# First five units of an attention and expert kernel: a new order of the work, other numbers of warming products, and the gate's tables on GpSimd

## The chip, the cores and the metric

The kernel runs on one core of one Trainium2 chip. A core has a matrix engine (TensorE, PE in the profile; the loading of its weights is a row of its own, PEld), a vector engine (VectorE, DVE), an engine for activations (ScalarE, ACT), a general engine (GpSimd, POOL) and one that mostly issues transfers (SyncE, SP). The metric is the device time of one execution in microseconds, as a median over runs.

## The reference

Eight batches of twelve heads of attention over 448 positions with 64 dimensions, in float32, then a layer of experts with one expert for each token. Cut to what matters:

```python
q_n, k_n = rmsnorm(q, g_q), rmsnorm(k, g_k)          # x / sqrt(mean(x*x) + 1e-6) * g
scores = (q_n @ k_n.T) / sqrt(64)                    # for each batch and head
attn = softmax(scores)
x = (attn @ v) laid out as 3584 tokens x 768
logits = x @ w_gate + modality_bias[modality_id]     # 8 experts
e = argmax(logits); gate_w = softmax(logits)[e]
out = gate_w * (relu(x @ w1[e]) @ w2[e])             # w1[e]: 768 x 1024, w2[e]: 1024 x 768
```

## The kernel before, in words

**Units.** The attention is cut into 48 units, each two heads of one batch. For a unit: its q and k are loaded (`load`); ScalarE squares them and VectorE sums the squares (`sq`, function `sumsq`); ScalarE, with GpSimd, makes the reciprocal roots (`rs`, function `rstd`, for several units at a time); the norms scale q and k (`norm`, one operation each); TensorE transposes them (`tr`, L750), and ScalarE and VectorE write the transposed q and k apart into a high and a low part, some of which SP moves to other partitions with transfers of 112 KB (L763). Then TensorE makes approximate products for the maxima (`sa`, seven of them, one for each of 128 rows; L822, L827), VectorE takes the row maxima, TensorE transposes these (`mt`, L838), and a transfer puts them beside the low part of q. The score products proper (`st`, L855, seven with two or four instructions each) subtract the maximum at once, ScalarE takes the exponential, GpSimd and VectorE sum parts of it (`csum`), and TensorE multiplies with the values (`av`, L894, four columns of a unit, two in one step and two singly). Later follow the row sums by TensorE (`sums`, L909), the gate's logits (`gates`, L916), their transposes (`recips`, L928) and the output's transposes (`xt`, L951).

**Steps.** The order of the work is written out. A step n counts seven to a unit: at step n = 7u + j TensorE makes `st` number j of unit u. The loop starts at step -22, and until step 0 there is no `st`, only preparation. Everything else has a step of its own: a default distance from the unit's first step (`PLAN['sa']` 14 steps ahead, for example), or a step in `PLAN['first']`, which holds exceptions, most of them for the units at the start. `when` (L1141) looks them up. In a step the loop (from L1171) issues, in this order: the warming products, `st`, `sa`, and (before step 0) two more warming calls, `av`, `sums`, `gates`, `tr`, `mt`; then the evacuations of what was made in earlier steps; squares, roots, sums, norms, loads. An engine takes its own instructions in the order in which they were issued, and each transfer stands in the queue of the engine that issues it, most of them in SP's.

**Warming.** `warm(n)` (L1093) makes n products of a constant 128 by 128 matrix with another, both float32, into a bank that nothing reads. How many calls it makes ahead of a step is in `PLAN['warm']`; `PLAN['warmn']` adds two after the `sa` of every step before step 0.

**The gate's tables.** `gate_consts` (L148) makes eleven small tables from the loaded modality numbers, the bias and four index patterns: 112 by 256 elements in the three large ones. They are first used in `route`, for the first batch, long after the start. In the kernel before, its operations are deferred: they go into a list (`slow`) after step 6, from which `pump` lets one or two be issued at certain points of a step.

**Transfers of the start.** At step -4 the loop issues the values of units 0 and 1 (`load_v`), the gate's weights, modality numbers and bias (`load_gate`), and a fill of the list of tokens in memory (`l_d`, 224 KB of zeros). From step 6 the values of unit i + 2 are loaded at the end of unit i.

**Norms.** A norm runs on GpSimd unless `PLAN['nv']` names it; it names the q norm of unit 0 and the k norm of unit 2, which run on VectorE.

After the attention follows the layer of experts in slots of 256 tokens, from about 600 us on. The change does not touch it.

Of the kernel before, what the change touches and what calls it, by code (L numbers as in the profile page):

```python
# [13 lines left out]
ALU = mybir.AluOpType  # L14
# [5 lines left out]
NT, DM, DFF, NE = 3584, 768, 1024, 8  # L20
# [46 lines left out]
def kernel(  # L67
# [69 lines left out]
    def load_gate():  # L137
        with nc.allow_non_contiguous_dma(reason="small gate tables"):
            for half in range(2):
                SY.dma_start(wg[64 * half : 64 * half + 64, :, 8 * half : 8 * half + 8],  # L140
                             w_gate.rearrange("(j h p) e -> h p j e", h=2, p=64)[half])
            SY.dma_start(modr, mod_id.bitcast(I32).rearrange("(b p w) -> p b w", b=B, p=CP))
        SY.dma_start(
            bia.rearrange("p m e -> p (m e)"),
            mod_bias.rearrange("m e -> (m e)").unsqueeze(0).to_broadcast([CP, 2 * NE]),
        )

    def gate_consts():  # L148
# [497 lines left out]
    if True:  # L646
# [406 lines left out]
        P = PLAN  # L1053
# [117 lines left out]
        for n in range(P["start"], NJ * NU):  # L1171
# [71 lines left out]
            if done and len(routed) < B - 1 and done[-1] >= (NP * len(routed) + 5) // 4:  # L1243
# [6 lines left out]
                    slow.append(("exp", lambda b=b: put_all(b)))  # L1250
                if b == NB1 - 1:
                    slow.append(("exp", tables1))
            if n == -4:
                load_v(0)
                load_v(1)
                load_gate()
                SY.dma_start(l_d.rearrange("(p r) w -> p (r w)", p=128), zt)
# [191 lines left out]
```

## Time and profile before

| | |
|---|---|
| median of three runs | 1127.89 us (1124.01 to 1129.05) |
| profiled execution | 1126.66 us |
| its span in the profile | 1124.8 us |
| first product of any kind | 1.50 us |
| first transpose (unit 0) | 9.88 us |
| step 0, first `st` of unit 0 | 42.16 us |
| first `st` of unit 1, 2, 3 | 50.47, 66.78, 77.48 us |
| last `st` instruction | 576.2 us |
| PE busy | 1074.1 us (95%) |
| VectorE, ScalarE, GpSimd busy | 863.4, 821.5, 659.5 us |

The span runs from the first to the last instruction. A busy TensorE is one with an instruction in it; at half clock the same work is busy twice as long, so the granted clock has to be read beside it. "Idle before" is time in which the engine had nothing in it, with what ended it behind the arrow. A float32 product leaves two records; a score product in the engine's reduced format leaves one.

### The profile page before, as it was taken

The page shows a single profiled execution, that of the slowest core. Times are in us where ns is not written, and L with a number is a line of the kernel's source. Part 1 is how long each engine was busy: PE and PEld are TensorE (multiplying, and loading weights), DVE is VectorE, ACT ScalarE, POOL GpSimd, SP SyncE. Part 2 cuts the span into 40 slices and gives each one's busy share as a digit, 9 for nine tenths or more (in the row PEclk, how much of TensorE's full clock was granted, in tenths as well). Part 3 has the DMA queues.
Part 4 walks back from the last instruction along what each step waited for, and adds up shares of the span by engine and source line. Part 5 has one row for each costly group of instructions (what it writes and reads, how often), then busy time and mean ns, then how long its engine had stood idle before and what let it go on. Part 6 is the DMA issues. An engine that isn't in the chain of part 4 may idle for free.

```text
span 1124.8 us, 19920 instructions
## 1 busy us (share of the span) xinstructions
PE 1074.1 (95%) x6678; PEld 837.5 (74%) x6678; DVE 863.4 (77%) x1604; ACT 821.5 (73%) x1545; POOL 659.5 (59%) x658
## 2 busy tenths in 40 slices
PE   7899999999999999998999999999999999999993
PEld 6655555555555555554569989999999999999991
DVE  4677788888889877899699977667777677776770
ACT  5678888878778787876677577667876678766870
POOL 4477677778777688787865474354234432445440
PEclk7999999999999999999999999999999999999997
DMA  6656676677666777665833202111170111111360
GB/s 169 150 137 163 147 180 167 158 172 172 154 169 147 172 161 182 146 145 111 239 124 92 48 29 66 29 58 57 43 267 29 57 58 43 33 40 57 100 207 8
DMA packets 127969, 131.79 MB, mean 117 GB/s; under 512 B 68891, under 2 KB 122607, under 8 KB 126320
## 3 DMA queue, kind: packets, MB, share of 16 engines
q1 hardware_dynamic: 110212, 88.58, 33.5%
q0 software_dynamic: 17616, 41.80, 11.8%
q8 instruction: 57, 0.93, 0.4%
q14 instruction: 56, 0.46, 0.1%
q10 hardware_dynamic: 28, 0.01, 0.0%
HBM read 148.74 MB, written 22.38 MB: 152 GB/s over the span
## 4 chain that ended last, share of the span: by engine, by line
PE 75%; DVE 11%; DMA 7%; ACT 2%; issue 2%; POOL 1%; SPq 1%; ACTq 0%; DVEq 0%; POOLq 0%
PE ph L485 18%; PE py L515 16%; PE av L894 12%; PE st L855 12%; PE sa L827 5%; DMA lt<-l_d,tb_li 4%; PE tr L750 3%; DVE w1w L52 2%; DVE at_hlw L52 2%; PE xt L951 2%; PE sm L909 2%; PE px L468 2%; DMA w1w<-xw 1%; DVE xw L52 1%; DVE w2lw L52 1%
## 5 line engine op out<-in xcount | busy, mean ns | idle before, releaser
L485 PE MATMUL ph<-xw,w1w 128*128 128x256 f32 x2016 | 247.6, 285 | 3.0 <-DVE hlw L52 2.3
L485 PEld LDWEIGHTS ph<-xw,w1w 128*128 128x128 f32 x2016 | 245.3, 193 | 5.0 <-DVE hlw L52 2.5
L52 DVE TENSOR_REDUCE at_hlw<-sa 128x1 f32<-128x448 f32 x336 | 206.6, 617 | 44.4 <-PE sa L827 25.5
L52 DVE TENSOR_TENSOR w1w<-r,w1w 128x256 fp32r<-128x256 f32 x360 | 221.4, 672 | 13.3 <-ACT w1w L52 13.3
L52 ACT CAST w1w<-r 128x256 fp32r<-128x256 f32 x360 | 225.3, 732 | 0.5 <-DVE tb_t L53 0.4
L855 PE MATMUL st<-w1w 128*128 128x448 f32 (+1 forms) x480 | 175.5, 415 | 1.6 <-ACT r2w L52 1.6
L52 ACT ACTIVATE r2w<-st 128x448 f32<-128x448 f32 x168 | 90.9, 543 | 49.7 <-PE st L855 42.0
L52 ACT ACTIVATE hhw<-ph 128x512 fp32r<-128x512 f32 x56 | 33.5, 598 | 124.5 <-PE ph L485 124.5
L827 PE MATMUL sa<-w1w 128*128 128x448 f32 (+1 forms) x288 | 110.9, 386 | 14.1 <-DVE at_hlw L52 7.1
L855 PEld LDWEIGHTS st<-w1w 128*128 128x128 f32 (+1 forms) x480 | 84.8, 190 | 44.2 <-ACT r2w L52 21.8
L52 POOL TENSOR_TENSOR r2w<-r2w 128x448 f32<-128x448 f32 (+1 forms) x72 | 82.9, 1151 | 57.6 <-DVE r2w L52 18.5
L515 PE MATMUL py<-w2lw,hhw 128*128 128x384 f32 x448 | 114.0, 335 | 0.0
L52 ACT ACTIVATE at_w2lw<-st 128x448 f32<-128x448 f32 x168 | 90.9, 543 | 23.3 <-PE st L855 17.3
L52 ACT CAST w1w<-xw 64x448 fp32r<-64x448 f32 x188 | 105.3, 561 | 2.0
L855 PE MATMUL st<-w1w,w2ha 65*128 65x448 f32 x288 | 100.7, 370 | 1.8 <-DMA w1w<-xw 1.7
L52 POOL TENSOR_TENSOR xrw<-r,at_hlw 112x512 f32<-112x512 f32 x94 | 96.9, 1050 | 1.0 <-PE tr L750 0.7
L52 POOL DMA_INDIRECT out_dram<-yw,lb_oi x22 | 25.3, 1152 | 122.2 <-ACT yw L52 112.3
L515 PEld LDWEIGHTS py<-w2lw,hhw 128*128 128x128 f32 x448 | 80.9, 188 | 0.0
L52 DVE SCALAR_TENSOR_TENSOR hlw<-ph,hhw 128x512 fp32r<-128x512 f32 x56 | 38.7, 690 | 53.4 <-ACT hhw L52 53.4
L827 PEld LDWEIGHTS sa<-w1w 128*128 128x128 f32 (+1 forms) x288 | 55.3, 192 | 27.4 <-DVE at_hlw L52 13.0
L52 POOL TENSOR_TENSOR r2w<-r2w,at_w2lw 64x448 f32<-64x448 f32 (+1 forms) x48 | 55.3, 1152 | 30.3 <-DVE r2w L52 11.3
L52 POOL DMA_INDIRECT xrw<-x_d,lb_x2i x24 | 30.3, 1261 | 67.0 <-DMA xrw<-x_d,lt 63.4
(296 smaller groups left out, 2284.9 us busy)
## 6 DMA issues: line engine op xcount, KB each, us to landing
w1w<-xw SPq DMA_DIRECT2D x312, 112.0 KB
r<-in_q_dram SPq DMA_DIRECT2D x48, 224.0 KB
r<-in_k_dram SPq DMA_DIRECT2D x48, 224.0 KB
w2ha<-xw SPq DMA_DIRECT2D x72, 112.0 KB
x_d<-at_w2hb SPq DMA_DIRECT2D x8, 672.0 KB
x_d<-yw SPq DMA_DIRECT2D x8, 672.0 KB
r2w<-in_v_dram SPq DMA_DIRECT2D x48, 96.0 KB
at_w2lw<-in_v_dram SPq DMA_DIRECT2D x48, 96.0 KB
```

The costliest lines, as they stand in the source:

```text
L52: return fn(*a, **kw)
L468: PE.transpose(ps[:, i, 128 * t : 128 * t + 128], xr[t][:, 2 * g + i], idn)
L485: PE.matmul(ps[:, i], lhsT=lt_, rhs=rt_[:, c], start=n == 0, stop=n == 17)
L515: PE.matmul(ps[n][:, :384], lhsT=lt_[:, j, 128 * t : 128 * t + 128], rhs=rt_[:, 384 * n : 384 * n + 384], start=j == 0 and m == 0, stop=j ...
L750: PE.transpose(sp[:, c], src[:, c], idn[:CP, :CP])
L827: PE.matmul(ps[:, :S], lhsT=t["qq"][r, h, a : a + 128], rhs=t["kk"][h][r], start=True, stop=True)
L855: PE.matmul(ps[:, :S], lhsT=l, rhs=t["qq"][:, h] if first else t["ql"][:, h], start=first and (j != 3 or h == 0), stop=not first and (j != ...
L894: PE.matmul(t["av"][64 * h : 64 * h + 64, :S], lhsT=vv[r, u % 3, j], rhs=t["p"][r, j], start=c == 0, stop=c == 3)
L909: PE.matmul(R[g][32 * i : 32 * i + 32, :S], lhsT=sel[:, m], rhs=T[u + i // 2]["cs"][:, i % 2], start=m == 0, stop=False, tile_position=(0, ...
L951: PE.transpose(ps[:CP, 128 * c : 128 * c + 128], T[u]["xt"][:, c * CP : (c + 1) * CP], idn)
```

## The change

It replaces two lines of the plan and edits two functions:

- The steps of `PLAN['first']` for units 0 to 5 are laid out anew. Squares, roots and norms of units 0 to 2 shift by up to five steps; their transposes by at most one; `sa` of units 0 and 1 comes one step earlier; for units 2 to 5 `sa`, `tr` and `mt` get explicit steps, of which both transposes of unit 3 (step 7 instead of 0 and 4) and `sa` of unit 3 (step 10 instead of 7) move most.
- `PLAN['warm']` has 168 calls instead of 32, 163 of them before step 0, and 55 + 22 + 7 + 3 + 1 in steps -22 to -18.
- `PLAN['nv']` is empty: all norms run on GpSimd.
- The loads of the start have steps of their own: the values of unit 0 at step -9, of unit 1 at step 1, the gate's loads at -7, the fill of `l_d` at 4.
- `gate_consts` runs on GpSimd, issued as a whole at step 3.

```diff
-PLAN = {... 'first': {('sq', 0): -22, ('sk', 0): -22, ('nk', 0): -21, ('nq', 0): -20, ('sq', 1): -20, ('sk', 1): -20, ('sq', 2): -19, ('sk', 2): -19, ('nk', 1): -18, ('nq', 1): -18, ('tk', 0): -18, ('tq', 0): -18, ('sa', 0): -14, ('tk', 1): -13, ('tq', 1): -11, ('sa', 1): -7, ('mt', 0): -6, ('tk', 2): -8, ('tq', 2): -8, ('nq', 2): -14, ('nk', 2): -14, ('nq', 3): -2, ('nk', 3): -1, ('sq', 3): -8, ('sk', 3): -8, ('sq', 4): -9, ('sk', 4): -9, ... ('tq', 3): 4, ('mt', 1): 0, ('nq', 5): 10, ... ('rs', 0): -21, ('rs', 2): -18, ... ('rs', 5): -7, ('mt', 2): 8, ... ('sa', 5): 22, ('rs', 7): 0, ('rs', 8): 6, ('mt', 4): 22, ('nk', 4): 4, ('ld', 9): 6, ('tk', 5): 15}, ... 'warm': {5: 2, -6: 16, -12: 4, -7: 2, -9: 4, -21: 4}, 'warmn': 2, ... 'nv': [(2, 1), (0, 0)], ...}
+PLAN = {... 'first': {('sq', 0): -22, ('sk', 0): -21, ('nk', 0): -19, ('nq', 0): -18, ('sq', 1): -20, ('sk', 1): -19, ('sq', 2): -19, ('sk', 2): -18, ('nk', 1): -16, ('nq', 1): -13, ('tk', 0): -18, ('tq', 0): -17, ('sa', 0): -15, ('tk', 1): -13, ('tq', 1): -11, ('sa', 1): -8, ('mt', 0): -6, ('tk', 2): -9, ('tq', 2): -9, ('nq', 2): -13, ('nk', 2): -10, ('nq', 3): -2, ('nk', 3): -3, ('sq', 3): -13, ('sk', 3): -11, ('sq', 4): -10, ('sk', 4): -9, ... ('tq', 3): 7, ('mt', 1): 2, ('nq', 5): 13, ... ('rs', 0): -20, ('rs', 2): -16, ... ('rs', 5): -5, ('mt', 2): 9, ... ('sa', 5): 23, ('rs', 7): 8, ('rs', 8): 16, ('mt', 4): 24, ('nk', 4): -1, ('ld', 9): 6, ('tk', 5): 14, ('sk', 5): -14, ('tk', 3): 7, ('tk', 4): 9, ('nk', 5): 7, ('sq', 5): -14, ('mt', 3): 17, ('nq', 4): 1, ('sa', 4): 17, ('tq', 4): 12, ('sa', 3): 10, ('sa', 2): 1, ('tq', 5): 18}, ... 'warm': {-22: 55, -21: 22, -20: 7, -19: 3, -18: 1, -16: 8, -15: 3, -13: 14, -10: 9, -9: 1, -8: 6, -6: 19, -4: 8, -3: 6, -2: 1, 5: 3, 7: 2}, 'warmn': 2, ... 'nv': [], ... 'lv': (-9, 1), 'lg': -7, 'lz': 4, 'gc': 3}
...
     def gate_consts():
-        V.tensor_copy(out=m1, in_=modr.rearrange("p b (c w) -> p (b c) w", w=2)[:, :, 0])
-        V.tensor_scalar(out=m0, in0=m1, scalar1=-1.0, scalar2=1.0, op0=ALU.mult, op1=ALU.add)
+        GP.tensor_copy(out=m1, in_=modr.rearrange("p b (c w) -> p (b c) w", w=2)[:, :, 0])
+        GP.tensor_scalar(out=m0, in0=m1, scalar1=-1.0, scalar2=1.0, op0=ALU.mult, op1=ALU.add)
...
-            if n == -4:
-                load_v(0)
-                load_v(1)
+            for u in range(2):
+                if n == P["lv"][u]:
+                    load_v(u)
+            if n == P["lg"]:
                 load_gate()
+            if n == P["lz"]:
                 SY.dma_start(l_d.rearrange("(p r) w -> p (r w)", p=128), zt)
+            if n == P["gc"]:
+                gate_consts()
...
-            if i == 0:
-                slow += deferred(gate_consts)
```

The other nine operations of `gate_consts` change their engine in the same way.

More of the change, by code (lines that the diff above doesn't have):

```diff
@@ L33 @@
 ET = mybir.EngineType
-PLAN = {'rtj': 6, 'rushat': 36, 'av': (1, 1, 4, 6), 'xt': 4, 'xte': (2, 5), 'sm': 2, 'la': 6, 'rc': 9, 'csv': (1,), 'csj': (3, 6), 'csd': (1, 1), 'cse': (2, 1), 'sa': 14, 'mt': 6, 'tk': 21, 'tq': 18, 'nq': 26, 'nk': 26, 'sk': 49, 'sq': 50, 'rs': 48, 'ld': 58, 'first': {('sq', 0): -22, ('sk', 0): -22, ('nk', 0): -21, ('nq', 0): -20, ('sq', 1): -20, ('sk', 1): -20, ('sq', 2): -19, ('sk', 2): -19, ('nk', 1): -18, ('nq', 1): -18, ('tk', 0): -18, ('tq', 0): -18, ('sa', 0): -14, ('tk', 1): -13, ('tq', 1): -11, ('sa', 1): -7, ('mt', 0): -6, ('tk', 2): -8, ('tq', 2): -8, ('nq', 2): -14, ('nk', 2): -14, ('nq', 3): -2, ('nk', 3): -1, ('sq', 3): -8, ('sk', 3): -8, ('sq', 4): -9, ('sk', 4): -9, ('sq', 6): -6, ('sk', 6): -4, ('sk', 7): -7, ('sq', 8): 5, ('sk', 8): 5, ('nk', 7): 15, ('nq', 9): 31, ('tq', 3): 4, ('mt', 1): 0, ('nq', 5): 10, ('mt', 8): 50, ('rs', 0): -21, ('rs', 2): -18, ('nq', 8): 35, ('rs', 5): -7, ('mt', 2): 8, ('nq', 7): 18, ('mt', 5): 30, ('sk', 9): 15, ('tk', 9): 43, ('mt', 6): 36, ('nq', 6): 13, ('sa', 5): 22, ('rs', 7): 0, ('rs', 8): 6, ('mt', 4): 22, ('nk', 4): 4, ('ld', 9): 6, ('tk', 5): 15}, 'rs0': {0: 0, 2: 1, 5: 0, 7: 0, 8: 2}, 'sastep': 1, 'start': -22, 'warm': {5: 2, -6: 16, -12: 4, -7: 2, -9: 4, -21: 4}, 'warmn': 2, 'early': 1, 'late0': 1, 'pmp0': 2, 'ramp': 10, 'pmp': (0, 0, 1, 1, 1, 0, 1), 'nv': [(2, 1), (0, 0)], 'pmpa': (1, 0, 1, 0, 1, 1, 1), 'rush': (1, 1, 1), 'ps': [], 'pa': [], 'rtr': 6, 'sml': 4}
@@ new lines @@
+PLAN = {'rtj': 6, 'rushat': 36, 'av': (1, 1, 4, 6), 'xt': 4, 'xte': (2, 5), 'sm': 2, 'la': 6, 'rc': 9, 'csv': (1,), 'csj': (3, 6), 'csd': (1, 1), 'cse': (2, 1), 'sa': 14, 'mt': 6, 'tk': 21, 'tq': 18, 'nq': 26, 'nk': 26, 'sk': 49, 'sq': 50, 'rs': 48, 'ld': 58, 'first': {('sq', 0): -22, ('sk', 0): -21, ('nk', 0): -19, ('nq', 0): -18, ('sq', 1): -20, ('sk', 1): -19, ('sq', 2): -19, ('sk', 2): -18, ('nk', 1): -16, ('nq', 1): -13, ('tk', 0): -18, ('tq', 0): -17, ('sa', 0): -15, ('tk', 1): -13, ('tq', 1): -11, ('sa', 1): -8, ('mt', 0): -6, ('tk', 2): -9, ('tq', 2): -9, ('nq', 2): -13, ('nk', 2): -10, ('nq', 3): -2, ('nk', 3): -3, ('sq', 3): -13, ('sk', 3): -11, ('sq', 4): -10, ('sk', 4): -9, ('sq', 6): -6, ('sk', 6): -4, ('sk', 7): -7, ('sq', 8): 5, ('sk', 8): 5, ('nk', 7): 15, ('nq', 9): 31, ('tq', 3): 7, ('mt', 1): 2, ('nq', 5): 13, ('mt', 8): 50, ('rs', 0): -20, ('rs', 2): -16, ('nq', 8): 35, ('rs', 5): -5, ('mt', 2): 9, ('nq', 7): 18, ('mt', 5): 30, ('sk', 9): 15, ('tk', 9): 43, ('mt', 6): 36, ('nq', 6): 13, ('sa', 5): 23, ('rs', 7): 8, ('rs', 8): 16, ('mt', 4): 24, ('nk', 4): -1, ('ld', 9): 6, ('tk', 5): 14, ('sk', 5): -14, ('tk', 3): 7, ('tk', 4): 9, ('nk', 5): 7, ('sq', 5): -14, ('mt', 3): 17, ('nq', 4): 1, ('sa', 4): 17, ('tq', 4): 12, ('sa', 3): 10, ('sa', 2): 1, ('tq', 5): 18}, 'rs0': {0: 0, 2: 1, 5: 0, 7: 0, 8: 2}, 'sastep': 1, 'start': -22, 'warm': {-22: 55, -21: 22, -20: 7, -19: 3, -18: 1, -16: 8, -15: 3, -13: 14, -10: 9, -9: 1, -8: 6, -6: 19, -4: 8, -3: 6, -2: 1, 5: 3, 7: 2}, 'warmn': 2, 'early': 1, 'late0': 1, 'pmp0': 2, 'ramp': 10, 'pmp': (0, 0, 1, 1, 1, 0, 1), 'nv': [], 'pmpa': (1, 0, 1, 0, 1, 1, 1), 'rush': (1, 1, 1), 'ps': [], 'pa': [], 'rtr': 6, 'sml': 4, 'lv': (-9, 1), 'lg': -7, 'lz': 4, 'gc': 3}
@@ L148, in gate_consts @@
     def gate_consts():
-        V.tensor_copy(out=m1, in_=modr.rearrange("p b (c w) -> p (b c) w", w=2)[:, :, 0])
-        V.tensor_scalar(out=m0, in0=m1, scalar1=-1.0, scalar2=1.0, op0=ALU.mult, op1=ALU.add)
+        GP.tensor_copy(out=m1, in_=modr.rearrange("p b (c w) -> p (b c) w", w=2)[:, :, 0])
+        GP.tensor_scalar(out=m0, in0=m1, scalar1=-1.0, scalar2=1.0, op0=ALU.mult, op1=ALU.add)
         shp = [CP, B * NCH, NE]
-        V.tensor_tensor(out=ball, in0=m0.unsqueeze(2).to_broadcast(shp),
+        GP.tensor_tensor(out=ball, in0=m0.unsqueeze(2).to_broadcast(shp),
                         in1=bia[:, 0:1, :].to_broadcast(shp), op=ALU.mult)
-        V.tensor_tensor(out=btmp, in0=m1.unsqueeze(2).to_broadcast(shp),
+        GP.tensor_tensor(out=btmp, in0=m1.unsqueeze(2).to_broadcast(shp),
                         in1=bia[:, 1:2, :].to_broadcast(shp), op=ALU.mult)
-        V.tensor_tensor(out=ball, in0=ball, in1=btmp, op=ALU.add)
+        GP.tensor_tensor(out=ball, in0=ball, in1=btmp, op=ALU.add)
         for tf, ti in iotas:
-            V.tensor_copy(out=tf, in_=ti)
-        V.tensor_scalar(out=ie8, in0=i_e[:, 0:NE], scalar1=float(NE), scalar2=None, op0=ALU.add)
-        V.tensor_scalar(out=i_ebase, in0=i_e[:, 0:NE], scalar1=float(NT), scalar2=None, op0=ALU.mult)
+            GP.tensor_copy(out=tf, in_=ti)
+        GP.tensor_scalar(out=ie8, in0=i_e[:, 0:NE], scalar1=float(NE), scalar2=None, op0=ALU.add)
+        GP.tensor_scalar(out=i_ebase, in0=i_e[:, 0:NE], scalar1=float(NT), scalar2=None, op0=ALU.mult)
     iotas = []
```

## The prediction

> **What bounds the kernel now.** I read the busy time by stretches first, cut where the work changes: 42.16 us is the first score product of unit 0 (step 0), 77.48 us that of unit 3 (step 21), 560 us is near the end of the attention. The columns are span, then busy time (and instructions) of PE, PEld, DVE, ACT and POOL, granted clock, DMA share, GB/s.
>
> ```profile
> 0.00:42.16 42.16, 34.79 (x188) 30.59 (x188) 23.63 (x55) 23.07 (x48) 15.52 (x38) 0.80 0.65 161
> 42.16:77.48 35.32, 29.28 (x143) 17.69 (x142) 25.65 (x47) 26.28 (x58) 25.20 (x31) 0.95 0.60 140
> ...
> 84.00:224.00 140.00, 139.94 (x759) 80.28 (x756) 112.22 (x214) 117.81 (x260) 104.34 (x112) 1.00 0.68 163
> 224.00:560.00 336.00, 326.68 (x1759) 186.59 (x1759) 283.01 (x573) 262.84 (x574) 264.35 (x277) 1.00 0.71 165
> 560.00:1124.80 564.80, 536.85 (x3807) 518.08 (x3803) 414.40 (x712) 385.52 (x596) 245.88 (x199) 0.98 0.23 72
> ```
>
> From 84 to 224 us PE has no idle time and the full clock, and until 560 us only 9.32 us of idle time in 336. So what moves unit 3 moves the end by about as much, and the question is when step 21 comes. The change works ahead of that point: 42.16 us of preparation and 35.32 us for three units. In the first, PE idles 42.16 - 34.79 = 7.37 us and runs at a mean clock of 0.80; in the second it idles 6.04 us.
>
> Next I read PE's instructions in order of time (start, duration, operation, count).
>
> ```profile
> 1.50 5.60 PE L1095 MATMUL warm<-idn,ones 128*128 128x128 f32 x28 [1.50 <-POOL idn masks.py:199]
> 9.88 1.76 PE L750 MATMUL tr<-idn,xrw 112*128 112x112 f32 x8 [2.78 <-POOL xrw L52]
> ...
> 32.53 4.18 PE L1095 MATMUL warm<-idn,ones 128*128 128x128 f32 x36
> 36.47 0.46 PE L827 MATMUL sa<-w1w 128*128 128x448 f32 x1
> 36.76 0.61 PE L1095 MATMUL warm<-idn,ones 128*128 128x128 f32 x4
> ...
> 42.16 0.45 PE L855 MATMUL st<-w1w 128*128 128x448 f32 x1
> ...
> 42.65 0.37 PE L827 MATMUL sa<-w1w 128*128 128x448 f32 x1
> 42.86 0.55 PE L750 MATMUL tr<-idn,xrw 112*128 112x112 f32 x4
> 43.24 0.28 PE L838 MATMUL mt<-idn,at_hlw 128*7 128x128 f32 x1
> ...
> 48.39 0.55 PE L750 MATMUL tr<-idn,xrw 112*128 112x112 f32 x4
> ...
> 53.86 0.62 PE L827 MATMUL sa<-w1w 128*128 128x448 f32 x1 [2.73 <-DMA w1w<-xw]
> ```
>
> Two things are to be seen. The records come in the order of the code, warming products among the others: they are not filler that gives way. And one call of `warm` leaves two records: from step -22 to -18 the code makes 4 + 5*2 = 14 calls, and 28 records stand before the first transpose. At full clock 36 records take 36.47 - 32.53 = 3.94 us, 0.109 us each, so **a call costs 0.219 us**.
>
> **The warming products.** Before step 0 the code now makes 30 calls by `warm` and 44 by `warmn` (two in each of 22 steps), 74 in all; afterwards 163 + 44 = 207. The 133 added calls are 133 * 0.219 = 29.1 us of PE. What they could fill is the idle time, 7.37 us, and what the half clock costs: a mean of 0.80 over 42.16 us is 16.9 us at half clock if the clock is either full or half, so 8.4 us. That is 15.8 us, about half of what is added.
>
> ```profile
> 15.00:20.00 5.00, 4.36 (x18) 3.54 (x19) 3.75 (x7) 3.35 (x9) 2.78 (x3) 0.64 0.53 117
> 20.00:25.00 5.00, 5.00 (x18) 3.79 (x18) 2.34 (x4) 1.32 (x3) 0.00 (x0) 0.50 0.93 219
> 25.00:30.00 5.00, 5.00 (x19) 3.73 (x18) 1.27 (x3) 3.10 (x7) 0.00 (x0) 0.50 0.56 128
> 30.00:35.00 5.00, 5.00 (x45) 4.97 (x46) 4.31 (x8) 3.49 (x8) 0.00 (x0) 0.99 0.48 129
> ```
>
> These rows show the half clock from about 16 to 30 us. The Trainium skill, "TensorE: Matmul & The Clock Gate", section "Part 1: The HAM clock gate", says that a window of about 3.4 us of activity gives the full clock and an idle one takes it away. By that rule the first 16 calls or so (an estimate: 3.4 us at 0.219) buy all that warming can buy at one place, and 77 calls in a row buy nothing more; it is a rule against this change.
>
> Now the sum, on PE's own stream. Steps -22 to -18 hold 98 calls (55 + 22 + 7 + 3 + 1 and ten of `warmn`) ahead of the first transpose, 196 records. The first 28 end as now, slow clock included, at 1.50 + 5.60 less the last one's tail of 0.28: 6.82 us. The other 168 take 18.4 us: **the first transpose starts at 25.2 us** where it now starts at 9.88. The remaining 109 calls are 23.8 us. Between them stand six groups of transposes (43.24 - 42.86 = 0.38 us each, 2.3), fourteen maximum products `sa` (36.76 - 36.47 = 0.29 each, 4.1) and one `mt` (0.03). So **step 0 starts at 25.2 + 30.2 = 55.4 us** at the earliest, against 42.16: 13.2 later.
>
> I take no wait of PE in this stretch. Of the edits that lie under this cover: both norms of unit 0 on GpSimd in a row (about 1.1 us more on its path), the squares, `rs` and norms of units 0 to 2 laid out anew, the value loads of unit 0 ahead of unit 2's moves on SP and the gate's loads behind them. The cover is the warming before the first transpose, 25.2 - 9.88 = 15.3 us, and the ten steps from unit 2's transposes (-9) to its first `sa` (step 1). ACT and DVE have 23.07 and 23.63 us of work in this stretch, which is to last 55. Without it the norms would cost their 1.1 us and each of these DMAs its issue, 0.4 to 0.7 us by the row of the fill, below.
>
> From step 0 to step 21 PE needs 29.28 us less what the half clock cost (a mean of 0.95 over 35.32 us, so 1.8), that is 27.5, and 0.7 for three more calls: 28.2. (Three `sa` of unit 4 leave this stretch and come in unit 3; 3 * 0.21 us, left out.) Without waits **step 21 comes at 83.6 us, 6.1 later than 77.48.**
>
> **The waits from step 0 to 21.** Now they are, by groups (last column idle time and what ended it):
>
> ```profile
> L855 PE MATMUL st<-w1w 128*128 128x448 f32 x24 | 9.9, 435 | 1.6 <-ACT r2w L52 1.6
> ...
> L827 PE MATMUL sa<-w1w 128*128 128x448 f32 x18 | 7.3, 405 | 4.4 <-DMA w1w<-xw 2.7 <-DVE at_hlw L52 1.7
> ```
>
> The 1.6 us behind ACT's exponentials stay, I take it: ACT has 26.28 us of work in a stretch that shall last some 30. Bounds 0 and twice that. The 2.7 us wait for unit 3's moves: from its second transposes (48.39) to its first `sa` (53.86) pass 5.47 us. In the new order both transposes stand at step 7 and `sa` at step 10. Between lie, at full clock, by these rows of unit 3:
>
> ```profile
> 79.10 1.73 PE L894 MATMUL av<-r2w 128*64 128x448 f32 x8
> 80.75 0.28 PE L838 MATMUL mt<-idn,at_hlw 128*7 128x128 f32 x1
> ...
> 81.49 0.98 PE L855 MATMUL st<-w1w 128*128 128x448 f32 x4
> 82.31 0.37 PE L827 MATMUL sa<-w1w 128*128 128x448 f32 x1
> ```
>
> Two columns of `av` 1.65, four products `st` at step 10 0.82, four more at steps 8 and 9 0.82, two groups of transposes 0.76, `mt` 0.03: 4.1 us. The wait is then 1.4 us. Lower bound 0. Upper bound: the fill of `l_d` (step 4) and the loads of unit 9 (step 6) now stand right ahead of these moves on SP's queue.
>
> ```profile
> r<-in_q_dram SPq DMA_DIRECT2D x48, 224.0 KB
> ```
>
> The fill, as it is issued now:
>
> ```profile
> 45.39 0.43 SPq L1257 DMA_DIRECT2D l_d<-yw  x1
> ```
>
> Three transfers of 224 KB (the fill has 448 words in 128 partitions, the same) at 140 GB/s are 4.8 us: at most 6.2 us of wait. The value loads of unit 1, now at step 1, are wanted at step 15 and lie under the products of unit 1.
>
> The gate's tables leave DVE. There they are 11 operations of 6.0 us together: the first, the three large ones and the last:
>
> ```profile
> 57.06 0.51 DVE L53 CAST m<-modr 112x32 f32<-112x32 int32 x1
> ...
> 60.19 1.21 DVE L53 TENSOR_TENSOR ball<-m,bia 112x256 f32<-112x256 f32 x1
> ...
> 61.33 1.35 DVE L53 TENSOR_TENSOR btmp<-m,bia 112x256 f32<-112x256 f32 x1
> ...
> 63.14 0.82 DVE L53 TENSOR_TENSOR ball<-ball,btmp 112x256 f32<-112x256 f32 x1
> ...
> 67.88 0.80 DVE L53 TENSOR_SCALAR i_ebase<-i_e 128x8 f32<-128x8 f32 x1
> ```
>
> They sit between the maxima for which `sa` waited 1.7 us; I take that wait to go (bounds 0 and 1.7 left). On GpSimd no row has them. Their loads are issued at step -7, ten steps ahead of them, so I take no wait of GpSimd for these. The nearest is the norm, which runs on both engines:
>
> ```profile
> L52 POOL TENSOR_TENSOR xrw<-r,at_hlw 112x512 f32<-112x512 f32 x8 | 8.5, 1063 | 0.7 <-PE tr L750 0.7
> ```
>
> On DVE the same operation is:
>
> ```profile
> 8.23 0.69 DVE L52 TENSOR_TENSOR xrw<-r,at_hlw 112x512 f32<-112x512 f32 x1 [1.63 <-POOL at_hlw L53]
> ```
>
> That is 1063 / 690 = 1.54, so 6.0 us (DVE's own) to 9.3 us. Behind them on GpSimd stand unit 0's second and third sums, then the norm of unit 5, which its transposes at step 14 want. GpSimd has 25.2 us of work in this stretch now; with the tables 31.2 to 34.5, in about 31.2 us (28.2 + 3.0). Taken as hidden, being at the edge at the lower price; at the upper 3.3 us late, on unit 5's transposes. The Trainium skill, "GPSIMD Engine Reference", section 3.1 "Elementwise", gives 1.96 as the ratio for a two-input add; by it the three large ones (3.4 us) would be 6.6 us, an estimate, and the whole at most 9.2, which changes nothing here.
>
> **Sum.** 6.1 + 1.6 + 1.4 = 9.1 us. On the profiled execution's 1126.66 us (span 1124.8) that is 1135.8; the median of the three runs, 1127.89, stands 1.2 above that execution, so I put the median afterwards at **1137 us**. With all waits at 0 it is 1134; with all at their upper ends, 6.1 + 3.2 + 6.2 + 1.7 + 3.3 = 20.5, it is 1148.
>
> **Rivals.** (1) *More waits*: unit 3's moves caught behind fill and loads and GpSimd late for unit 5, 14 to 20 us in all, 1142 to 1148. For it speaks the order on SP; against, that a transfer has been given the whole rate of the stretch as its price. 14%. (2) *Not slower*: the place is the steady stretch. The PE has 9.32 us of idle time between 224 and 560 us, where an operand came late; work of the first units that is done 13 us deeper into the loads could leave each later unit further ahead, and these waits go. With all waits before step 21 gone as well: 1127.89 + 6.1 - 9.3 = 1124.7. It decides from 0.5 us given back on, since 5.6 us (0.5%, about what a measurement of this kernel can tell from no change) is still no difference. Against it: from unit 6 on, steps of both orders agree but for two root computations, so nothing keeps the lead. 13%. (3) *The clock pays*: warming runs only while PE would wait, the first transpose stays at 9.88, and 8.4 us of half clock are gained: 1119. The skill's clock gate rule, read without PE's order, gives this. It needs 133 calls in 7.4 us of idle time, which holds 34. 5%. (4) *The change doesn't cost what its calls say*: if a call were one record, 207 * 0.109 = 22.7 us less, step 0 would come at 32.7 and the end near 1114. 28 records for 14 calls speak against it. 2%.
>
> **Chances.** Forecast 66%. Range 1131 to 1144: below it lie (3), (4) and about half of (2), above it the far end of (1), some 2 in 10. Faster by over 0.5%: (3), (4) and 2 of (2), 9%. Within 0.5% (1122.3 to 1133.5): the rest of (2), 11%. Slower: 80%.
>
> **What would show it.** The first transpose near 25 us with 196 warming records ahead of it; full clock from about 6 us on; step 0 at 55 to 56 us with no idle row above 1 us before it; step 21 at 85 to 88 us; unit 3's first `sa` still waiting for a DMA; no gate table on DVE, and no `sa` waiting 1.3 us for DVE there; from then on the intervals between units as before. The forecast is wrong if the first transpose is not held up by the warming, if step 21 comes before 80 us, or if idle time after 224 us changes by more than 3 us.

## The result and the profile after

| | before | changed |
|---|---|---|
| median | 1127.38 us (8 runs, 1124.01 to 1130.13) | 1140.66 us (8 runs, 1135.29 to 1146.50) |
| ratio | | 1.0122, interval 1.0096 to 1.0148 |
| profiled execution, its span | 1126.66, 1124.8 us | 1146.50, 1144.7 us |

The changed kernel is slower by 13.3 us, 1.2%. Its profiled execution is the slowest of its eight, 5.8 us above their median, so the profile overstates the loss: 19.8 us stand between the two profiled executions. The ratios here and below leave out four slow executions, which the medians hold: one of the kernel before (2600 us), the profiled one with the gate's tables back on VectorE (1759 us), and one each of the kernels with one burst and with no warming (1136 and 1138 us).

The stretches of the changed kernel, cut at the same events as before: 57.06 us is step 0, 86.25 us step 21, 108.75 us step 35 (the first `st` of unit 5). Columns as in the prediction: span, busy time of PE, PEld, DVE, ACT and POOL, granted clock, DMA share, GB/s.

```profile
0.00:57.06 57.06, 55.57 (x453) 53.40 (x454) 23.12 (x54) 23.29 (x48) 17.27 (x41) 1.00 0.53 128
57.06:86.25 29.19, 27.70 (x147) 17.18 (x145) 18.23 (x32) 24.14 (x55) 27.37 (x41) 1.00 0.61 144
86.25:108.75 22.50, 21.61 (x109) 12.06 (x107) 17.60 (x29) 18.85 (x44) 14.98 (x18) 1.00 0.67 157
```

The kernel before, units 3 and 4 alone (step 21 to step 35), which the prediction did not show:

```profile
77.48:97.73 20.25, 20.25 (x106) 11.51 (x104) 14.45 (x25) 18.13 (x41) 13.44 (x16) 1.00 0.68 161
```

So step 0 came 14.90 us later (57.06 against 42.16), 6.13 us of that were won back until step 21 (29.19 us instead of 35.32), and 2.25 us were lost again in units 3 and 4. At step 35 the changed kernel is **11.0 us** behind. From there to unit 18 the distance stays as it is: 108.20 us against 119.22 at unit 6 (step 42), 240.49 against 251.79 at unit 18. Between units 18 and 47 this execution loses 5.6 us more; the second profile, below, does not.

TensorE in order of time in the changed kernel, and below the group of `sa` in the stretch from 57.06 to 86.25 us (count, busy, mean ns, idle time before and what ended it).

```profile
1.49 23.81 PE L1095 MATMUL warm<-idn,ones 128*128 128x128 f32 x196 [1.49 <-POOL idn masks.py:199]
25.14 0.55 PE L750 MATMUL tr<-idn,xrw 112*128 112x112 f32 x4
...
29.38 0.46 PE L827 MATMUL sa<-w1w 64*128 64x448 f32 x1
29.77 0.71 PE L1095 MATMUL warm<-idn,ones 128*128 128x128 f32 x4
30.41 0.47 PE L827 MATMUL sa<-w1w 64*128 64x448 f32 x1
...
57.06 0.45 PE L855 MATMUL st<-w1w 128*128 128x448 f32 x1
...
70.08 0.44 PE L827 MATMUL sa<-w1w 128*128 128x448 f32 x1 [1.19 <-DMA w1w<-xw]
...
86.25 0.68 PE L855 MATMUL st<-w1w 128*128 128x448 f32 x2
```

```profile
L827 PE MATMUL sa<-w1w 128*128 128x448 f32 x15 | 5.6, 372 | 1.2 <-DMA w1w<-xw 1.2
```

The 98 calls leave 196 records, and the transposes that start at 9.88 us in the kernel before stand behind them until 25.14. Unit 3's wait for its moves is 1.19 us here where it was 2.73. The waits of `st` for ACT (1.6 us) and of `sa` for DVE (1.7 us) of the kernel before are gone; 0.28 us of one `av` behind ACT are new.

The gate's tables on GpSimd, the first, the three large ones and the last of eleven operations:

```profile
59.92 0.20 POOL L52 CAST m<-modr 112x32 f32<-112x32 int32 x1
...
60.51 0.63 POOL L52 TENSOR_TENSOR ball<-m,bia 112x256 f32<-112x256 f32 x1
61.09 0.63 POOL L52 TENSOR_TENSOR btmp<-m,bia 112x256 f32<-112x256 f32 x1
61.80 0.74 POOL L52 TENSOR_TENSOR ball<-ball,btmp 112x256 f32<-112x256 f32 x1
...
63.46 0.24 POOL L52 TENSOR_SCALAR i_ebase<-i_e 128x8 f32<-128x8 f32 x1
```

All eleven take 3.7 us together, where they took 6.0 on DVE.

### The profile page after: what moved, and what is told of

Its sections match the earlier page's. It is cut to its first block, busy times and chain, and to the rows that moved or that the text cites. A ratio compares the mean times of both kernels' runs of the same rounds, so it can differ in the third digit from the quotient of the medians.

```text
span 1144.7 us, 20462 instructions
## 1 busy us (share of the span) xinstructions
PE 1100.4 (96%) x6950; PEld 862.7 (75%) x6950; DVE 858.6 (75%) x1591; ACT 821.7 (72%) x1545; POOL 663.0 (58%) x671
## 4 chain that ended last, share of the span: by engine, by line
PE 78%; DVE 9%; DMA 6%; ACT 2%; issue 2%; POOL 1%; SPq 0%; ACTq 0%; DVEq 0%; POOLq 0%
PE ph L485 18%; PE py L515 16%; PE st L855 12%; PE av L894 12%; PE sa L827 5%; PE warm L1095 4%; DMA lt<-l_d,tb_li 3%; PE tr L750 3%; DVE w1w L52 3%; DMA w1w<-xw 2%; PE xt L951 2%; PE px L468 2%; PE sm L909 2%; DVE at_hlw L52 2%; PE sa L822 1%
## 5 line engine op out<-in xcount | busy, mean ns | idle before, releaser
L52 DVE TENSOR_TENSOR w1w<-r,w1w 128x256 fp32r<-128x256 f32 x360 | 221.7, 673 | 13.3 <-ACT w1w L52 13.3
L52 DVE TENSOR_REDUCE at_hlw<-xrw 112x8 f32<-112x512 f32 x96 | 64.8, 676 | 5.5 <-ACT xrw L52 5.4
```

The lines of the kernel that those rows point to most:

```text
L52: return fn(*a, **kw)
```

## The experiments

Each time is a median, with the ratio to the kernel before in runs on the same chip. That kernel's own median was 1125.57 us beside the first four runs, 1124.58 beside the next four and 1126.0 beside the last four.

**Theory and rival.** "The new order" is short for everything in the change but the warming: steps, norms, loads and the gate's tables. Theory A is the prediction's: each warming call is paid on TensorE's stream before step 0, the new order repays part of it by waits that go, and what is left at step 21 arrives at the end. Rival B: the new order, the tables or what the delay does later bear the loss, or the waits go only because of the delay.

### The new order with the old warming

```diff
 # changed kernel
-'warm': {-22: 55, -21: 22, -20: 7, -19: 3, -18: 1, -16: 8, -15: 3, -13: 14, -10: 9, -9: 1, -8: 6, -6: 19, -4: 8, -3: 6, -2: 1, 5: 3, 7: 2}
+'warm': {5: 2, -6: 16, -12: 4, -7: 2, -9: 4, -21: 4}
```

> The changed kernel with the warming calls of the kernel before (32 instead of 168); order, loads, norms and gate's tables stay new. Theory (the warming calls are paid for in full and the new order itself saves the waits after step 0): the first transpose comes back to about 10 us, step 0 to 40 to 44 us, the stretch from step 0 to 21 stays at 29 to 30 us, step 21 comes at 70 to 73 us and the time is 1120 to 1124 us, faster than before. Rival (the waits after step 0 went only because the long preparation gave the data time): that stretch grows back to 33 to 36 us and the time is 1126 to 1130 us, as before.

Measured: 1121.09 us, ratio 0.9962 (0.9940 to 0.9984). With the old warming the new order is faster than the kernel before. Its stretches to steps 0, 21 and 35, and its group of `sa` from step 0 to step 21:

```profile
0.00:36.77 36.77, 30.95 (x188) 27.19 (x188) 21.72 (x51) 22.55 (x48) 14.38 (x36) 0.86 0.72 180
36.77:69.20 32.43, 28.23 (x140) 16.85 (x138) 19.89 (x34) 24.53 (x56) 29.61 (x46) 0.95 0.66 149
69.20:92.21 23.01, 21.78 (x110) 12.06 (x108) 18.12 (x29) 18.85 (x44) 15.47 (x18) 1.00 0.66 154
```

```profile
L827 PE MATMUL sa<-w1w 128*128 128x448 f32 x15 | 6.0, 400 | 3.1 <-DMA w1w<-xw 2.9 <-issue 0.2
```

Step 0 comes at 36.77 us where the profile before had 42.16, and step 35 at 92.21 where it had 97.73. Not all of that is the order's. The two runs with a delay in the steady part, below, leave the start of the kernel before as it was, so there are two more traces of it. Their stretches to step 0:

```profile
0.00:38.84 38.84, 31.47 (x187) 28.06 (x188) 24.33 (x55) 22.96 (x48) 15.52 (x38) 0.87 0.71 175
0.00:39.72 39.72, 31.61 (x187) 28.09 (x188) 24.33 (x55) 22.85 (x48) 15.52 (x38) 0.87 0.68 172
```

The same code reached step 0 at 42.16, 38.84 and 39.72 us, with granted clocks of 0.80, 0.87 and 0.87, and step 35 at 97.73, 95.98 and 98.04 us. Against these three the order (36.77 us, and 36.35 in the second run) gains 2.1 to 5.8 us at step 0 and 3.8 to 6.4 at step 35. The expected 29 to 30 us from step 0 to step 21 did not come, nor did the rival's 33 to 36: it took 32.43. Two waits for moves stand there, 2.9 us of unit 3's `sa` and 0.8 of an `st`. Under the long warming unit 3's wait is shorter (1.19), and in the old order it goes under the same delay (next section), so this part of the saving does hang on the delay; but in the old start it was 2.73, 1.22 and 1.61 us from trace to trace. The waits of `st` for ACT and of `sa` for DVE, which all three traces of the old start have, stay away, so they went by the order.

The same kernel was run a second time with the last four, as the version that may beat both:

> The changed kernel with the old warming calls once more, beside the trimmed one on one chip. Theory (the new order alone saves some 5 us at the start): 0.994 to 0.998 of the kernel before again, unit 5 at 91 to 93 us. Rival (the 4.5 us were that chip's luck): within 0.3% of the kernel before.

Measured: 1120.10 us, ratio 0.9939 (0.9919 to 0.9958); step 35 at 91.67 us. **This version beats both kernels**, by 0.4 to 0.6% against the one before.

### The old order with the new warming

```diff
 # kernel before
-'warm': {5: 2, -6: 16, -12: 4, -7: 2, -9: 4, -21: 4}
+'warm': {-22: 55, -21: 22, -20: 7, -19: 3, -18: 1, -16: 8, -15: 3, -13: 14, -10: 9, -9: 1, -8: 6, -6: 19, -4: 8, -3: 6, -2: 1, 5: 3, 7: 2}
```

> The kernel before with only the warming calls of the changed one (168 instead of 32); order, norms, loads and gate's tables stay old. Theory: 98 calls stand before the first transpose again, step 0 comes at 55 to 57 us, and with the old order the waits from step 0 to 21 stay near 6 us, so 33 to 35 us for that stretch, step 21 at 88 to 92 us and 1139 to 1144 us. Rival (cover alone takes the waits away): step 0 to 21 in 29 to 30 us, step 21 at 85 to 86 us, 1134 to 1137 us.

Measured: 1146.63 us, ratio 1.0171 (1.0136 to 1.0205), later than either expectation. The stretches, and the groups from step 0 to step 21 that waited:

```profile
0.00:57.93 57.93, 56.43 (x453) 54.27 (x454) 24.55 (x55) 23.29 (x48) 15.60 (x38) 1.00 0.50 120
57.93:93.60 35.67, 30.10 (x149) 18.16 (x148) 27.25 (x47) 25.85 (x58) 25.24 (x31) 0.95 0.55 131
93.60:113.86 20.26, 20.26 (x106) 11.50 (x105) 14.44 (x25) 17.88 (x41) 13.46 (x16) 1.00 0.71 167
```

```profile
L855 PE MATMUL st<-w1w 128*128 128x448 f32 x24 | 9.9, 433 | 2.7 <-ACT r2w L52 2.7
...
L827 PE MATMUL sa<-w1w 128*128 128x448 f32 x18 | 7.2, 401 | 2.9 <-DVE at_hlw L52 2.7 <-ACT xrw L52 0.2
```

The delay alone removes unit 3's wait for its moves, but not the waits for ACT and DVE (2.7 us each): 35.67 us from step 0 to step 21, as long as in the kernel before (35.32). In the old order the warming costs 1146.63 - 1125.57 = 21.1 us, in the new one 1138.69 - 1120.10 = 18.6 to 1140.66 - 1121.09 = 19.6. The order gains 4.5 to 5.9 us under the old warming (1125.57 - 1121.09, 1126.0 - 1120.10) and 6.0 to 7.9 under the new (1146.63 less 1140.66 or 1138.69). These medians come from different chips; by the ratios to the kernel before on the same chip the warming costs 1.7% in the old order and 1.6 to 2.1% in the new (19 us, and 18 to 23), and the order gains 0.4 to 0.6% under the old warming and 0.3 to 0.5% under the new (3 to 7 us). The two effects add to within some 3 us, and that the waits go only because of the delay holds for one of them.

### The gate's tables back on DVE

```diff
 # changed kernel
-        GP.tensor_copy(out=m1, ...)          # and the other ten operations
+        V.tensor_copy(out=m1, ...)
...
-            if n == P["gc"]:
-                gate_consts()
...
+            if i == 0:
+                slow += deferred(gate_consts)
```

> The changed kernel with the gate's tables on the vector engine again, deferred from step 6 as before; all else new. Theory (the move takes away up to 1.7 us of waits for row maxima, GpSimd carries the tables for nothing): 1 to 2 us slower than the changed kernel, 1141.5 to 1143 us, and a wait of sa for the vector engine near the tables. Rival (the tables never were on the path): within 0.7 us of the changed kernel, 1140 to 1141.4.

Measured: 1138.53 us, ratio 1.0101 (1.0068 to 1.0133), beside 1.0122 and 1.0146 for the changed kernel. The 1 to 2 us that were expected to be lost are not seen: the engine of the tables makes no difference that these runs can tell, and none of the 13 us. Whether `sa` waits for DVE again near the tables no trace here shows, so which part of the new order took that wait away stays open.

### Thirty-five warming calls fewer

```diff
 # changed kernel
-'warm': {-22: 55, ...
+'warm': {-22: 20, ...
```

> The changed kernel with 20 calls instead of 55 at step -22, all else as changed: 35 calls fewer, 35 * 0.219 = 7.7 us. Theory (calls are paid one for one): first transpose at 17.4 us instead of 25.1, step 0 at 49.4, unit 5 at 101 us, and 6 to 9 us less than the changed kernel, 1130 to 1134 us. Rival (the long warming gave the data time, so waits come back): less than 4 us gained, step 0 to 21 above 31 us.

Measured: 1135.72 us, ratio 1.0075 (1.0048 to 1.0102). The start in order of time, and the stretches to steps 0, 21 and 35:

```profile
1.49 16.70 PE L1095 MATMUL warm<-idn,ones 128*128 128x128 f32 x126 [1.49 <-POOL idn masks.py:199]
18.02 0.55 PE L750 MATMUL tr<-idn,xrw 112*128 112x112 f32 x4
```

```profile
49.95:79.06 29.11, 27.57 (x146) 17.18 (x144) 18.23 (x32) 23.99 (x55) 27.33 (x41) 1.00 0.65 154
79.06:101.55 22.49, 21.60 (x109) 12.07 (x107) 17.55 (x29) 18.84 (x44) 14.94 (x18) 1.00 0.69 157
```

The first transpose comes 7.12 us earlier (25.14 to 18.02), step 0 7.11 and step 35 7.2 us earlier than in the first profile of the changed kernel, and 7.7 to 7.8 us than in the second (next section; 25.77 for the transpose). 35 calls at 0.219 us are 7.7. The clock and the stretch from step 0 to step 21 (29.11 us) are what they were: the 35 calls cost their full price, bought nothing, and no wait of the new order came back without them. By the ratios 0.5 to 0.7% of the time was saved, 5 to 8 us.

### The changed kernel once more

Nothing is edited but a comment.

> The changed kernel once more, unaltered, for a second profile of it. Theory (of the 19.9 us between the first two profiles some 11 us are the start and the rest differs from execution to execution): first transpose at 25.1 us, step 0 at 57 us, step 21 at 86 us and unit 5 at 108 to 109 us again, but the stretch from unit 5 to the last score product (484.3 us in the first profile of the changed kernel, 478.5 before) and the stretch after it differ by 2 us or more from the first; 1138 to 1142 us. Rival (the later loss belongs to the change): both later stretches again within 1.5 us of the first profile's.

Measured: 1138.69 us, ratio 1.0146 (1.0106 to 1.0185); profiled execution 1139.20, span 1137.4 us.

```profile
0.00:57.69 57.69, 56.20 (x453) 54.03 (x454) 23.37 (x54) 23.05 (x48) 17.25 (x41) 1.00 0.52 126
57.69:86.81 29.12, 27.59 (x147) 17.18 (x145) 18.23 (x32) 24.00 (x55) 27.36 (x41) 1.00 0.62 145
86.81:109.31 22.50, 21.61 (x109) 12.08 (x108) 17.55 (x29) 18.84 (x44) 14.91 (x18) 1.00 0.67 157
```

The start repeats to 0.6 us. From the first `st` of unit 5 to that of unit 47 this execution took 469.0 us, the first one 475.8 (584.51 - 108.75), the kernel before 469.9 (567.61 - 97.73). So the 5.9 us that the first profile lost there belong to that execution and not to the change.

### A delay in the steady part

The delay is put at step 35 of the kernel before, where it cannot change the start: 50 products of 128 columns, and then, with as much time in fewer instructions, 13 products of 512 columns (the tile is shaped 128 by 4 by 128 there).

```diff
 # kernel before, ahead of st of step 35
+            if n == 35:
+                wp2 = ps_t.tile([128, 512], F32, tag="t", name="warm2")
+                for _ in range(50):
+                    PE.matmul(wp2[:, :128], lhsT=ones, rhs=idn, start=True, stop=True)
```

> The kernel before with 50 warming products (10.9 us by 0.219 us each) put into step 35, the first of unit 5, in a bank of their own: a pure delay of TensorE inside the steady stretch. Theory (a delay there goes to the end one for one): +10.9 us, 1137 to 1140 us, the idle time of TensorE after it as before within 3 us. Rival A (units further ahead shrink the later waits): below +8 us, under 1135.5. Rival B (a later start meets more waits, as the profile of the changed kernel has 16.9 us more at its last score product but 11.0 us at unit 5): above +12.5 us, over 1140.

```diff
+                for _ in range(13):
+                    PE.matmul(wp2, lhsT=ones, rhs=idn.unsqueeze(1).to_broadcast([128, 4, 128]), start=True, stop=True)
```

> The pure delay in step 35 of the kernel before again, now by 13 products of 512 columns (13 * 0.85 = 11.1 us) instead of 50 of 128, so with 52 instructions fewer than a quarter of the other's 200. The delay by 50 cost about 19 us; its profile shows 11 us in the place, 5.8 us in which TensorE waited for nothing shown (issue) at the first product of the last small slot, and a rest. Theory (the 5.8 us come with the place of the instructions in the stream, the delay itself goes to the end one for one): no such wait, 1136 to 1139.5 us. Rival (a later start really costs more further on): 1142 to 1147 us as before, with or without this wait.

Measured: 1144.87 us, ratio 1.0163 (1.0128 to 1.0198), for the narrow products; 1134.59, ratio 1.0110 (1.0080 to 1.0140), for the wide ones. The two delays in the traces, the narrow ones' first, and then two instructions near the end of the run with narrow products:

```profile
95.98 11.43 PE L1182 MATMUL warm<-idn,ones 128*128 128x128 f32 x100
...
1111.01 0.45 PE L587 MATMUL qx<-idn,xrw 32*128 32x32 f32 x2 [3.19 <-issue]
1114.07 0.61 PE L587 MATMUL qx<-idn,xrw 32*128 32x32 f32 x4 [2.61 <-issue]
```

```profile
98.04 11.43 PE L1182 MATMUL warm<-idn,ones 128*128 128x512 f32 x26
```

Both delays last 11.43 us. The wide ones cost 10.0 us by the medians (12.4 by the ratio): a delay in the steady part arrives at the end about one for one, as theory A has it. The narrow ones cost 19.3 us (18.3 by the ratio), which A does not explain. Their trace shows 5.8 us in which TensorE waited in the last slot of the experts for nothing that the profile names ("issue"); the run with wide products has no such wait there. From the first expert product of the last full slot to the end pass 73.0 us with the narrow ones and 67.5 with the wide, 5.5 us of the difference. What differs between the two edits is the number of TensorE's instructions, 100 records or 26, and the width of each; the two were timed on different chips.

### The warming cut to one burst, or to nothing

```diff
 # changed kernel
-'warm': {-22: 55, -21: 22, ... 7: 2}, 'warmn': 2
+'warm': {-22: 16, 5: 2}, 'warmn': 2          # first kernel
+'warm': {}, 'warmn': 0                       # second kernel
```

> The changed kernel with 16 warming calls at step -22 and 2 at step 5 instead of 168; the two calls in each step before step 0 stay. Theory (calls are paid for where no wait of TensorE lies under them; 16 fill the 4 us before the first transpose, the others of the run with the old warming, 16 at step -6 and 14 more, are paid for): full clock from about 5 us on, first transpose at 10.5 us, step 0 at 29 to 33 us, step 0 to 21 in 32 to 35 us, step 21 at 62 to 67 us, 1114 to 1118 us, 7 to 11 us faster than the kernel before. Rival (the data are not there earlier than in the run with the old warming, so waits take the place of the calls): step 21 at 68 to 70 us and 1120 to 1122 us.

> The changed kernel without any warming call. Theory (under the calls lie now the chains of transposes, evacuations and transfers, and the half clock): TensorE runs at half clock until it is dense, waits stand where the calls were, step 0 comes at 27 to 33 us and the time is within 3 us of the run with 18 calls and two a step. Rival A (the warming that is left is still paid for): 4 us or more faster than that run. Rival B (the half clock lasts into the dense stretch): 4 us or more slower.

Measured: 1130.41 us, ratio 1.0054 (1.0025 to 1.0083), with one burst; 1128.09, ratio 1.0039 (1.0006 to 1.0071), with none. Neither time that was expected for one burst (1114 to 1118 us, or 1120 to 1122) came. Both reach step 35 earlier than the kernel with the old warming (90.60 and 88.41 us, against 92.21 and 91.67), and yet their medians are 7 to 10 us above its. Two rows of the kernel without warming, and its first stretch:

```profile
20.56 0.74 PE L827 MATMUL sa<-w1w 64*128 64x448 f32 x1 [0.59 <-DVE at_hlw L52]
...
31.85 0.57 PE L855 MATMUL st<-w1w 128*128 128x448 f32 x1
```

```profile
0.00:31.85 31.85, 13.99 (x40) 8.22 (x40) 21.30 (x51) 22.54 (x48) 14.46 (x36) 1.00 0.79 201
```

`sa` takes 0.74 us here and 0.47 in the changed kernel: 0.74 is what it took in the kernel before at 21.19 us, where the clock column reads 0.50, so TensorE ran at the low clock up to step 0 (the 1.00 in the clock column is no measurement, since the first change of the clock in this trace is at 34.8 us). It hardly mattered, with 13.99 us of work in 31.85. In these traces warming does not bring the start forward: of all kernels with the new order this one is the first at step 0, by 3 us or more. What the two kernels lose, they lose behind unit 47, where nothing was edited: from there to the end pass 564.55 us without warming and 564.52 in the second run with one burst (next section), against 558.29 and 555.93 with the old warming. The first profile with one burst, the fastest of its twelve executions at 1119.09 us, has 559.24.

### The number of TensorE's instructions

The kernel with one burst has 28 records fewer than the kernel before (6650 against 6678). Fourteen products of one row and one column, at step -22, bring it to 6678 again.

```diff
 # kernel with one burst
+            if n == -22:
+                for _ in range(14):
+                    PE.matmul(wps[0:1, 0:1], lhsT=ones[:, 0:1], rhs=idn[:, 0:1], start=True, stop=True)
```

> The trimmed kernel (16 calls at step -22, 2 at step 5) once more. Its first profile was 7 us ahead of the kernel before at unit 5 and at the end, but its 12 timed runs had a median 5.8 us over that of the kernel before. Theory (a wait at the last small slot, called issue, 2 to 6 us, comes with the number of TensorE instructions ahead of it, 6650 products here against 6678, and eats the start's gain): such a wait again, and the time 3 to 8 us over the run with the old warming. Rival (that chip's scatter): the time is that of the old warming less 1 to 4 us.

> The trimmed kernel with 14 products of one row and one column at step -22, so that TensorE has as many products (6678) as in the kernel before and in the run with the old warming, which had no issue wait. Theory (the number places the later code): no issue wait at the last small slot, first transpose at 10 to 11.5 us, unit 5 at 90 to 92 us and 1117 to 1122 us. Rival (the loss of the trimmed kernel has another cause): 1127 to 1132 us as without the padding.

Measured: 1129.39 us, ratio 1.0021 (0.9997 to 1.0046), without the fourteen; **1120.95, ratio 0.9952 (0.9927 to 0.9977), with them**. Work was added and 8.4 us were gained. The last slot's first products, in the run without them and then in the run with them:

```profile
1094.40 0.82 PE L587 MATMUL qx<-idn,xrw 32*128 32x32 f32 x5 [2.25 <-DVE ig L52]
1097.91 0.21 PE L587 MATMUL qx<-idn,xrw 32*128 32x32 f32 x1 [2.68 <-issue]
```

```profile
1093.95 0.96 PE L587 MATMUL qx<-idn,xrw 32*128 32x32 f32 x6 [2.32 <-DVE ig L52]
```

The wait named issue is gone. Over all kernels it goes with the number of TensorE's records. The last column is the time from the first expert product of the last full slot to the end of the span:

| records of TensorE | kernels | wait named issue at `qx` | that stretch |
|---|---|---|---|
| 6526, 6650 (twice), 6778 | no warming, one burst, narrow delay | 2.2 to 5.8 us | 72.1 to 73.0 us |
| 6678 (four times), 6704, 6880, 6950 (three times) | before, old warming twice, padded, wide delay, 35 fewer, changed twice, old order | none | 67.3 to 70.1 us |

So some kernels lose 2 to 6 us near the end by where their instructions come to lie, whatever else they do. That explains about 4 us of the 8.4 (72.1 against 68.1). Where the rest lies stays open: the padded kernel's profiled execution (1125.76 us) is 4.8 us above its median, so its trace cannot show it.

The profile has a queue of its own for instructions, and its transfers of 16 KB go with TensorE's records: 56 of them with 6526 and 6650 records, 57 with 6678 and 6704, 58 with 6778 and 6880, 59 with 6950. In the run with one burst it carries one transfer in the 3.2 us around the wait (from 1094.8 to 1098 us; queue, packets, MB, share of 16 engines):

```profile
q8 instruction: 1, 0.02, 3.1%
```

The padded run has such a transfer near the same products as well (one from 1093.9 to 1096 us) without the wait. Two things stand in the traces. Each of the five waits named issue at `qx` begins within 0.4 us of the start of one such transfer and ends 1.25 to 1.57 us after the end of it; the waits of the first `qx` in the other traces, which the profile puts down to VectorE, end 1.54 to 1.68 us after one too. And the place counts. Ahead of the first `qx` TensorE's sequencer stands in a branch, for 3.3 to 4.6 us in every trace. Counting all of TensorE's instructions in a trace (products, weight loads, the sequencer's own) from its start, the product that waits a second time behind the branch stands at a remainder of 219 by 256 in three traces and of 220 in the fourth, 4 to 10 instructions behind the first `qx`. In the kernels without the wait the first `qx` has remainders from 9 to 157, so the next such place is 62 instructions or more away. A fetch of TensorE's instructions that comes too late when a new block of 256 begins right behind the branch fits all of this, and the fourteen products moved the place (from 209 to 9 for the first `qx`) and took the wait away. That the transfers are TensorE's is inferred from their number; why the medians differ by more than the wait is not shown.

## Why the prediction was right, and where it was off

The direction was right: forecast 1137 us, measured 1140.66 and 1138.69. Point by point:

- **A call costs 0.219 us and stands in TensorE's order**: right. 196 records, the first transpose at 25.14 us (forecast 25.2); with 35 calls fewer, 7.12 us earlier. The rival that a call is half as dear (1114) and the one that warming gives way and the clock pays (1119) fall with it.
- **The clock**: the Trainium skill, "TensorE: Matmul & The Clock Gate", section "Part 1: The HAM clock gate", has it that one busy window of about 3.4 us opens the gate. The trace agrees: the full clock is first recorded 5.0 us into the span of the changed kernel, 3.5 us after its first product, and with 35 calls fewer the stretch after step 0 keeps its clock of 1.00 and its 29.11 us, so these 35 bought nothing. Not every later call did nothing for the clock: with the old warming in the new order it was 0.86 up to step 0 and 0.95 from there to step 21, with the new warming 1.00 in both. But what it gave was less than it cost.
- **Step 0 at 55.4 us**: 57.06 and 57.69, mis-sized by 1.7 to 2.3 us. The term is "fourteen maximum products `sa` (36.76 - 36.47 = 0.29 each)". That row is one with 128 rows; six of the fourteen are unit 0's with 64 rows. From one of these to the next with two calls between pass 30.41 - 29.38 = 1.03 us, less 0.44 for the calls 0.59, 0.3 us more than taken. Over the six, measured so up to the next row that is no call, it is 0.42 to 0.68 each, 1.5 us more than taken in all.
- **Step 0 to step 21**: 28.2 + 3.0 = 31.2 forecast, 29.19 measured. "The 1.6 us behind ACT's exponentials stay, I take it" was wrong: they went, by the order, since the old order keeps them under the same delay (2.7 us). The wait of unit 3's first `sa` came in the size worked out (1.4 forecast, 1.19), but its cause is not settled: the second profile and the one with 35 calls fewer put the same wait (1.25 and 1.26) down to ACT's writing of `xw` and not to the moves. The wait for DVE went, as taken, and the three `sa` of the next point are missing from PE's work. The errors before and after step 0 cancel, which is luck: step 21 at 86.6 forecast, 86.25 and 86.81 measured.
- **"Three `sa` of unit 4 leave this stretch and come in unit 3; 3 * 0.21 us, left out"**, and units 3 and 4 as before: wrong by 2.25 us. PE's busy time there is 1.36 us longer. The only group with another count is `sa`, 15 in place of 12, so that is 0.45 for each of the three if all of it is theirs, where 0.21 was taken; 0.89 us are idle, most of it one wait of `sa` for DVE. All kernels with the new order show 22.5 to 23.0 us there, the old order under the same delay 20.26, so it is the order's. The group in the changed kernel from 86.25 to 108.75 us:

```profile
L827 PE MATMUL sa<-w1w 128*128 128x448 f32 x15 | 5.6, 384 | 0.8 <-DVE at_hlw L52 0.8
```

- **The sum at the end of the start**: 9.1 us forecast. At unit 5 it is 11.0 and 11.6 us against the one trace that the prediction had, and 10.7 to 13.3 against all three traces of the old start. The medians differ by 13.3 and 14.1. So one trace of a start leaves some 2.5 us of this lag open, and most of the gap to the medians may be no more than that. What is left, up to 3 us, was not found; from unit 47 to the end the two profiles of the changed kernel take 3.0 and 1.9 us more than the one before, but all kernels without a wait named issue lie between 555.9 and 560.2 us there, so this stretch does not decide it.
- **The gate's tables**: bounded by 6.0 to 9.3 us on GpSimd from the norm's ratio of 1.54; they took 3.7, below the lower bound. The row taken was the wrong one: a norm of 512 columns says little of products of 256 with broadcast operands. The Trainium skill, "GPSIMD Engine Reference", section 3.1 "Elementwise", gives 1.96 as the ratio of GpSimd's time to VectorE's for a two-input add of 2048 columns. These rows do not agree with it: 0.63 / 1.21 = 0.52, 0.63 / 1.35 = 0.47 and 0.74 / 0.82 = 0.90, for 256 columns. It cost nothing that the runs can tell either way, as taken.
- **Afterwards as before**: right for the steady part. The rival that idle time after 224 us is given back falls: in the stretch from 235 to 577 us, which stands for 224 to 560 before, it is 342.00 - 331.43 = 10.6 us in the first profile, against 9.32 in about the same work.

```profile
235.00:577.00 342.00, 331.43 (x1764) 188.60 (x1764) 282.56 (x573) 263.88 (x574) 265.28 (x277) 0.99 0.70 162
```

- **More waits (1142 to 1148)**: did not come. Unit 3's moves were not caught behind the fill and the loads, and GpSimd was not late.

## What to carry to other kernels

A product that warms TensorE stands in its stream like any other: count the records ahead of the first real work, multiply, and compare with the idle time that they can fill. Here the new order gained 3 to 8 us, the added products cost some 20, and the two only came apart when each was run alone; an edit with a good and a bad half is worth splitting before it is judged. One profile is one execution: the same start took 38.84 to 42.16 us here, so a gain of a few us at one event wants more than one trace of the kernel before. And a few us in a kernel of this length can come from where the instructions lie alone (8.4 us between two medians here, 4 of them in the traces), so an experiment that adds or removes instructions needs a partner with the same number.

## What was not expected of the hardware

Fourteen products of one element took 8.4 us off the time (1129.39 to 1120.95), and 100 narrow records cost 9 us more than 26 wide ones of the same duration (the losses are 19.3 and 10.0 us, on two chips, and the intervals of the ratios overlap a little), with waits of 2 to 6 us near the end that the profile puts down to nothing. GpSimd was not the slower engine everywhere: the products with broadcast operands took 0.63 us there and 1.21 to 1.35 on VectorE. (A profile's spans on GpSimd are rough.) And a maximum product with 64 rows between products with 128 held the stream for 0.42 to 0.68 us, one with 128 rows for 0.29 (36.47 to 36.76 in the kernel before).
